# Two channels per kernel matmul in an S4 convolution kernel, with a new written order

## The chip, the cores and the metric

The kernel runs on one core of a Trainium2 chip. The metric is the device time of one execution in microseconds (us); the median of several runs is given with the lowest and the highest. One more execution was taken with the hardware profiler: its own time, its span (first to last instruction) and its trace are what is read here. The engines are called as the profile calls them: PE is TensorE (matmuls), PEld the weight loads of PE, DVE is VectorE, ACT is ScalarE, POOL is GpSimd, SP is SyncE, which issues most of the DMAs.

## The reference

The input `A_u` is 2048 rows of 512 channels. With `xn` the layer-normalised rows, the output is `x + s * g`:

```python
# _A_ref: long convolution, one kernel of 2048 taps per channel, 128 modes each
P = jnp.exp(logdA[:, :, None] * l[None, None, :])      # logdA = dt * (A_re + i A_im)
K = jnp.einsum("dn,dnl,dn->dl", Cc, P, dB).real
...                                                    # Kf, Uf: real FFTs of length 4096 of K and xn
Yf = Uf * Kf[None, :, :, :]
y = ...                                                # inverse FFT, first 2048 rows, + u * Dskip
# _B_ref: one row only goes through a gated layer
r = x @ w_r
idx = jnp.argsort(-r, axis=-1)[:, :C]                  # C = 1
y = (_silu(x_sel @ w_gate) * (x_sel @ w_up)) @ w_down  # times sigmoid of r at that row
return x + upd                                         # upd is y at that row, 0 elsewhere
...
x = A_u
xn = _layernorm(x, axis=-1)
s = _A_ref(xn, A_A_re, A_A_im, A_B_re, A_B_im, A_C_re, A_C_im, A_log_dt, A_Dskip)
g = _silu(_B_ref(xn, B_w_r, B_w_gate, B_w_up, B_w_down))
return x + s * g
```

## The kernel before

Everything is in SBUF, and the Fourier transforms are matmuls with constant tables.

*Front.* The rows arrive as X, are normalised (statistics on DVE, L791 and L794; XN on DVE, L815, or ACT, L814), and go out again and come back transposed as XZN by 16 DMAs on SP. XN is also written to a scratch tensor in DRAM, `scr_g`, from which the gate is read near the end. Beside it the parameters are loaded to STG and turned into weights: from sines and cosines SG, four products SL and two sums WC, 128x512 each, which PE turns over (PB<-DPF,WC) into MB. The forward transform of XN takes two steps, CB,XZN to AU and AU with F2A and F2B to BIG. A router picks one row; its gated layer streams weights through WRING, SMB and the small row GRW, which is added to `scr_g` at the chosen row by an indirect DMA on POOL.

*Kernel.* The 512 channels go in four quarters, called (h, s) in the code, 128 channels each. For a quarter, exponentials E and sines SN over 32 lags and powers GG over 20 base rows are made by ACT and DVE; `kgen_mm` multiplies them for each channel by itself: 32 columns of E (then of SN) as weights, 20 columns of GG moving, so 32 lags by 20 rows for one channel. Four channels sit side by side in the four column groups of the array, at (0, 32j). That is 256 matmuls a quarter and 1024 in all. KE takes them out of PSUM, and small matmuls (KE,CB) bring them to KX with the channels in order. `spec` multiplies KX by the table FD, 20 matmuls a group and 8 groups a quarter (KX,FD), KF takes a group out of PSUM (L624 on ACT, L625 on DVE), and DVE multiplies it into the spectrum of XN (BIG<-BIG,KF). FD is loaded in four parts of 8 of its 32 blocks, so each quarter uses the last part in its last two groups. `inv_a` is the first step back, with CB,BIG to CC.

*End.* `fin(h)` is the second step back, for half of the channels in five blocks: matmuls CC,FB, then DVE multiplies the block in PSUM with the gate, TB<-PB,G, adds the residual XR, and the block is stored. The gate G0 is read from `scr_g` after the chosen row is in it, and ACT makes it silu(gate) in four pieces (L591, G<-G).

*Order.* No engine picks its work at run time. `_Graph.op` records every operation with what it reads and writes; the table `ORDER` (L368) lists, for each engine, the numbers of its operations in the order in which they are issued; `schedule` puts them so and `emit` writes a semaphore wait where an operation needs another engine's or a DMA's. An evacuation of PSUM made by `evac` can stand on either ACT or DVE, whichever list has its number. Some helpers record many kinds of operation on one line: `mm` L642 all matmuls, `tt` L596 all two-input operations, `act` L591, `dma` L659, `memset` L628. A buffer's place in SBUF is fixed (RG, RM and so on are offsets), so two buffers at one place order each other.

Of the kernel before, what the change touches and what calls it, by code (L numbers as in the profile page):

```python
# [7 lines left out]
ACT = mybir.ActivationFunctionType  # L8
# [8 lines left out]
KB = 1024  # L17
# [310 lines left out]
def tables():  # L328
# [33 lines left out]
    for q in range(2):  # L362
# [11 lines left out]
        0-1 4 3 20 5 15 23-25 28 27 26 30-32 29 34 375 385 377 398-399 388 396 379 390-391 383 394 386 371 395 382 380 397 389 372 374 370 384 376
        393 378 392 387 400 373 381 49 48 50 47 175 36 44 51-52 403 58 133 131 134 412 53-54 57 55 76 56 75 46 416 405 81 79-80 82 425 433 427-428
        424 417 426 88 85 92 87 408 407 411 430 423 229 404 413 429 406 419 233 235 422 435 431 418 239 409 420 241 243 245 356 421 434 414 249 251
        253 255 257 259 432 410 415 263 265 267 269 271 584 583 273 275 277 279 615 601 605 281 283 491 285 287 593 494 289 291 661 293 591 611 613
        603 597 609 607 589 599 595 585 587 482 546 558 664 570 572 578 574-575 559-560 568 553 573 580 577 569 550 579 554 562 565 571 567 561 676
        566 555 557 556 552 563 576 564 551 608 755 752 594 616 590 598 586 588 610 758 596 612 604 592 606 602 600 614 764 685 767 549 770 332 689
        687 693 701-702 773 704 777 781 800 695 694 806 782-783 812 789-790 792 818 886 833 892 835 834 820 898 826 824 836 906 908 912 847 846 863  # L380
# [12 lines left out]
        889-890 895-896 822 901 893 902 838 842 839 841 899 840 844 904 851 910 858 845 865 859 866 873 852 874 921 914 922 915 928 935 929 936
        943-944""",
    gpsimd="""
        402 401 298 302 300 296 225 304 306 308 310 581-582 312 314 316 318 320 322 324 326 334 336 338 340 342 344 346 348 350 352 354 365""",
    tensor="""
        33 35 43 45 228 230 198-200 232 234 201 236 238 204 240 242 208 244 210 246 248 250 215 252 217 254 256 258 222 262 264 266 268 270 486 272
        274 487 276 278 490 488 280 282 489 284 286 226 493 288 290 660 292 537 297 299 538 541 301 303 539-540 663 666 544 672 669 678 305 675 307
        748 309 681 311 754 313 751 315 684 317 757 319 760 321 763 323 766 325 769 327 688 686 335 337 692 698 339 699 341 696 343 345 697 700 772  # L400
        347 703 349 776 351 793 353 780 355 799 360 690 796 774 805 778 784-785 788 811 802 786-787 808 791 814 879 882 817 885 888 891 894 821 900
        897 837 819 825 823 843 903 905 850 907 909 857 911 864 920 871-872 913 934 927 941-942""",
# [7 lines left out]
def build(nc, A_u, A_A_re, A_A_im, A_B_re, A_B_im, A_C_re, A_C_im, A_log_dt, A_Dskip,  # L410
# [51 lines left out]
    with g.ctx:  # L462
# [78 lines left out]
        E = g.buf("E", RE, [32, 256], BF16)  # L541
        SN = g.buf("SN", RS_, [32, 256], BF16)
# [12 lines left out]
        KE = [g.buf(f"KE{i}", RKE + 1280 * i, [20, 32], BF16) for i in range(2)]  # L555
# [351 lines left out]
        def exps(h):  # L907
            g.stage = f"exps{h}"
            hs = slice(256 * h, 256 * h + 256)
            for i in range(31):  # L910
                act(E(E.a[i]), AR(AR.a[hs]), ACT.Exp, scale=float(128 + LAGS[i]), table="exp")
            memset(PO, E(E.a[31]), 1.0)

        def sines(h):
            g.stage = f"sin{h}"
            hs = slice(256 * h, 256 * h + 256)
            th = TH(TH.a[hs])
            memset(PO, SN(SN.a[0]), 0.0)
# [322 lines left out]
```

## Time and profile before

| | |
|---|---|
| median of 3 runs, lowest, highest | 198.55 us, 197.79, 199.75 |
| the profiled execution's own time | 196.53 us |
| its span | 194.6 us |
| mean granted clock of PE | 0.891 |
| busy PE / PEld / DVE / ACT / POOL | 131.6 / 116.2 / 158.5 / 124.7 / 18.3 us |
| matmuls in the trace | 2960 |
| moved by DMA | 31.64 MB, mean 163 GB/s |
| bytes of instructions fetched (queue q8) | 23 packets, 0.38 MB |

Busy time is when at least one instruction of an engine was in work; register, branch and DMA-issuing instructions do not count. Matmuls overlap, so the mean of one (some 220 ns) is much longer than the distance between two, and busy time over count is the better measure. A granted clock of 0.50 means that PE was held to half speed in that stretch. The profile's groups read "line engine operation out<-in shapes xcount | busy, mean ns | idle before, releaser".

### The profile page before, as it was taken

Reading aid. Unit: us, or ns where it says so; the run is one execution under the profiler, and the core shown is the slowest. Engines: PE = TensorE matmul, PEld = TensorE weight load, DVE = VectorE, ACT = ScalarE, POOL = GpSimd, SP = SyncE. Lnnn points to the kernel's source line nnn. Section 1 sums busy time; section 2 is a strip of 40 time slices with the busy share of each in tenths; the row PEclk is TensorE's granted clock in tenths of the full one; section 3 lists DMA queues with packets and bytes.
Section 4 is the critical chain, followed back from the end, with each engine's and each line's share of the span. In section 5 each row is a group of like instructions: output and inputs, shape, how many; then the busy total and the mean of one; then the engine's idle time right before and its main releaser. Section 6 shows DMA issues by size and latency. Waiting matters only on the chain.

```text
span 194.6 us, 6818 instructions
## 1 busy us (share of the span) xinstructions
PE 131.6 (68%) x2960; PEld 116.2 (60%) x2960; DVE 158.5 (81%) x395; ACT 124.7 (64%) x246; POOL 18.3 (9%) x37
## 2 busy tenths in 40 slices
PE   0114040069786799935599997999999999958450
PEld 0003030069654567735589997989979899847330
DVE  0999998996799999991479999996947478949881
ACT  0699999994999969990099998243311339834000
POOL 6000000000002000022103433230010000000000
PEclk9999999999999979965599999856997999999755
DMA  5995069991000197999502444220296699980775
GB/s 162 383 384 236 2 132 149 159 389 38 0 0 2 19 308 177 331 365 301 121 0 76 129 132 126 84 88 20 59 229 153 205 421 316 201 158 20 158 150 121
DMA packets 24449, 31.64 MB, mean 163 GB/s; under 512 B 11012, under 2 KB 19332, under 8 KB 23652
## 3 DMA queue, kind: packets, MB, share of 16 engines
q1 hardware_dynamic: 16974, 22.79, 42.3%
q10 hardware_dynamic: 5958, 4.19, 9.5%
q0 software_dynamic: 1488, 4.23, 7.3%
q8 instruction: 23, 0.38, 0.8%
q14 instruction: 6, 0.05, 0.1%
HBM read 20.72 MB, written 4.20 MB: 128 GB/s over the span
## 4 chain that ended last, share of the span: by engine, by line
PE 40%; DVE 25%; ACT 15%; issue 8%; DMA 7%; SPq 2%; ACTq 0%
PE PB L642 40%; ACT E L591 5%; DVE TT L596 4%; DVE BIG L596 4%; DMA CF<-c_cf 4%; DVE GG L596 3%; DMA XZN<-XN 3%; DVE KF L625 3%; SPq L659 2%; DVE TB L596 2%; ACT BIG L624 2%; ACT XN L814 1%; ACT L591 1%; DVE E L596 1%; DVE AU L625 1%
## 5 line engine op out<-in xcount | busy, mean ns | idle before, releaser
L642 PE MATMUL PB<-KX,FD 128*128 128x128 bf16 x640 | 42.9, 229 | 0.7 <-DVE KF L625 0.5
L642 PEld LDWEIGHTS PB<-KX,FD 128*128 128x128 bf16 x640 | 39.7, 104 | 1.4 <-DVE KF L625 0.7
L596 DVE TENSOR_TENSOR TT<-GG,MB 128x512 bf16<-128x512 bf16 (+2 forms) x64 | 27.8, 462 | 0.1
L591 ACT ACTIVATE E<-AR 128x256 bf16<-128x256 f32 x62 | 19.4, 401 | 7.2 <-PE PB L642 7.2
L596 DVE TENSOR_TENSOR BIG<-BIG,KF 128x1024 bf16<-128x1024 bf16 x32 | 21.0, 685 | 2.7 <-issue 1.6
L642 PE MATMUL PB<-GG,SN 128*32 128x20 bf16 x512 | 19.7, 221 | 4.8 <-issue 4.8
L642 PE MATMUL PB<-CB,XZN 128*128 128x256 bf16 x64 | 11.7, 325 | 16.0 <-DMA XZN<-XN 13.4
L642 PE MATMUL PB<-GG,E 128*32 128x20 bf16 x512 | 19.7, 223 | 3.5 <-issue 3.2
L624 ACT ACTIVATE CC<-PB 128x1024 bf16<-128x1024 f32 (+1 forms) x14 | 12.4, 900 | 14.5 <-PE PB L642 14.5
L642 PEld LDWEIGHTS PB<-GG,E 128*32 128x32 bf16 x512 | 17.9, 167 | 5.7 <-issue 4.3
L642 PEld LDWEIGHTS PB<-GG,SN 128*32 128x32 bf16 x512 | 18.3, 169 | 4.5 <-issue 4.5
L642 PE MATMUL PB<-CB,BIG 128*128 128x128 bf16 x256 | 20.7, 240 | 0.5 <-ACT CC L624 0.3
L642 PEld LDWEIGHTS PB<-CB,BIG 128*128 128x128 bf16 x256 | 18.7, 153 | 1.4 <-issue 0.4
L642 PEld LDWEIGHTS PB<-CB,XZN 128*128 128x128 bf16 x64 | 8.5, 181 | 18.1 <-ACT MB L777 13.7
L596 DVE TENSOR_TENSOR GG<-TT 128x256 bf16<-128x256 bf16 (+2 forms) x66 | 18.1, 303 | 0.0
L625 DVE CAST KF<-PB 128x512 bf16<-128x512 f32 x17 | 11.6, 684 | 7.8 <-PE PB L642 7.8
L624 ACT ACTIVATE BIG<-PB 128x1024 bf16<-128x1024 f32 x16 | 15.7, 1059 | 1.8 <-PE PB L642 1.8
L624 ACT ACTIVATE KF<-PB 128x512 bf16<-128x512 f32 x15 | 8.9, 599 | 11.4 <-PE PB L642 11.3
L624 ACT ACTIVATE AU<-PB 128x1024 bf16<-128x1024 f32 x13 | 12.8, 1048 | 2.6 <-PE PB L642 2.6
L791 DVE BATCH_NORM_STATS2 ST<-X 128x6 f32<-128x512 bf16 x16 | 10.2, 673 | 4.3 <-DMA X<-in_A_u_dram 4.3
L596 DVE TENSOR_TENSOR TB<-PB,G 128x1024 bf16<-128x1024 f32 (+1 forms) x10 | 9.9, 1006 | 3.9 <-PE PB L642 3.9
L642 PE MATMUL PB<-DPF,WC 128*128 128x128 f32 x16 | 4.1, 441 | 11.2 <-DVE WC L596 11.2
(129 smaller groups left out, 240.2 us busy)
## 6 DMA issues: line engine op xcount, KB each, us to landing
FD<-c_fd SPq DMA_DIRECT2D x4, 1280.0 KB, 7.5
X<-in_A_u_dram SPq DMA_DIRECT2D x4, 512.0 KB, 5.5
XZN<-XN SPq DMA_DIRECT2D x16, 128.0 KB, 4.7
scr_g<-XN SPq DMA_DIRECT2D x4, 512.0 KB, 7.1
BIG<-BIG ACTq DMA_DIRECT2D x4, 512.0 KB, 6.7
G<-scr_g SPq DMA_DIRECT2D x1, 2048.0 KB
FB<-c_fb SPq DMA_DIRECT2D x1, 2048.0 KB, 15.7
XR<-in_A_u_dram SPq DMA_DIRECT2D x4, 512.0 KB, 13.4
```

Source lines behind the costliest of these rows:

```text
L591: g.op(AC, lambda e: e.activation(out=out.ap, in_=in_.ap, func=func, **kw), w=[out], r=r, cost=cost(AC, out, 0.834) - (20 if in_.buf.space ...
L596: g.op(eng, lambda e: e.tensor_tensor(out=out.ap, in0=a.ap, in1=b.ap, op=op), w=[out], r=[a, b], cost=cost(eng, out, rate))
L624: g.op(AC, lambda e: e.activation(out=out.ap, in_=in_.ap, func=ACT.Copy), w=[out], r=[in_], cost=cost(AC, out, 0.834) - 20, alt=(DV, lambd ...
L625: alt=(DV, lambda e: e.tensor_copy(out=out.ap, in_=in_.ap), cost(DV, out, 1.042)))
L642: ins = e.matmul(o_.ap, lhsT=l_.ap, rhs=r_.ap, start=st, stop=sp, **kw)
L659: fn = lambda e: e.dma_start(dst, src)
L791: g.op(DV, lambda e, b=b: e.bn_stats(ST6(ST6.a[b]).ap, X0(X0.a[b]).ap), w=[ST6(ST6.a[b])], r=[X0(X0.a[b])], cost=593)
L814: flex(ov, [iv, mv_, nv, rv], lambda e, ov=ov, iv=iv, nv=nv, rv=rv: e.activation(out=ov.ap, in_=iv.ap, func=ACT.Identity, bias=nv.ap, scal ...
```

## The change

The kernel's lines move by one or two: `mm` is L643, `tt` L597, `dma` L660, `evac` L625 and L626.

1. `kgen_mm` takes two channels in one matmul: 64 columns of E or SN (32 lags of two channels) as weights and 40 columns of GG (20 rows of the same two) moving. Half of each result is the product of unlike channels and is not used. There are 128 matmuls a quarter, 512 in all, at (0, 64jp). E and SN are laid out as [2, 32, 128], so that the columns are 64 elements apart (256 before). The results need twice the PSUM, so a quarter is made in two halves on the same two banks, each with its own KE evacuation; KE is one buffer for all quarters, and the matmuls KE,CB pick every second column of the identity to sort the channels.
2. The six products SL and WC are on POOL.
3. In `fin(1)` the blocks 0, 2 and 4 are copied by ACT from PSUM to YB in SBUF (bf16), and DVE multiplies from there.
4. XR lies where MB was (RM) and is recorded ahead of FB and G0; TB, V4, VM and YB lie where GG was. G0 comes in two loads, one for each half of the channels, and the silu pieces follow the halves.
5. All lists of `ORDER` are new. X comes first on SP. All 16 XN are on DVE (12 before, 4 were on ACT); all 16 AU evacuations are on ACT (13 before); of BIG's 16 evacuations one is on DVE; of KF's 32 casts 9 are on DVE (17 before).

PE first, where the first quarter's spectrum products meet the second quarter's kernel matmuls. Names: GG,E and GG,SN are the kernel matmuls, KX,FD the spectrum products, AU,F2B the second step of the forward transform. Before:

```order
L642 MATMUL PB<-AU,F2B 128x4x64 x16
L642 MATMUL PB<-KX_120,FD 128x2x64 x20
L642 MATMUL PB<-AU,F2B 128x4x64 x8
L642 MATMUL PB<-GG,E 32x20 x4
L642 MATMUL PB<-GG,SN 32x20 x4
```

and now, ahead of the first half of these kernel matmuls (the last two rows go on 16 times) the first fence, and at the end of the half, before the next, the second:

```order
L643 MATMUL PB<-KX_119,FD 128x2x64 x20
L643 MATMUL PB<-AU,F2B 128x4x64 x8
L643 MATMUL PB<-KX_119,FD 128x2x64 x20
L643 MATMUL PB<-AU,F2B 128x4x64 x16
L643 MATMUL PB<-GG,E 64x40 x2
L643 MATMUL PB<-GG,SN 64x40 x2
```

```order
L643 MATMUL PB<-GG,SN 64x40 x2
L643 MATMUL PB<-KX_119,FD 128x2x64 x20
L643 MATMUL PB<-AU,F2B 128x4x64 x8
L643 MATMUL PB<-KX_119,FD 128x2x64 x20
L643 MATMUL PB<-GG,E 64x40 x2
```

Before, one group of KX,FD stood ahead of the 256 kernel matmuls, which were broken only by the small matmuls of the router and the gated layer. Now two groups stand ahead of the first 64 and two between the halves; the other four follow the second half.

SP at the end of the program: the issue of the last loads. BIG is the exchange of spectrum halves, GRW the gated row, G the gate, FB the table of `fin`. Before:

```order
L659 DMA BIG<-BIG 64x2x1024
L659 DMA GRW<-UPD 8x1x64
L659 DMA G_132<-scr_g 128x8192
L659 DMA FB<-c_fb 128x8192
L659 DMA XR<-in_A_u_dram 32x32x256 x4
L659 DMA out_dram<-XR 32x8x128 x3
```

and now:

```order
L660 DMA BIG<-BIG 64x4096
L660 DMA XR<-in_A_u_dram 32x32x256 x4
L660 DMA BIG<-BIG 64x4096
L660 DMA GRW<-UPD 8x1x64
L660 DMA FB<-c_fb 128x8192
L660 DMA G_131<-scr_g 128x2x2048 x2
L660 DMA out_dram<-XR 32x8x128 x10
```

XR moved from the last of the loads to the first; FB stands between the gated row and the gate, which has two issues.

ACT near its end, where the gate's silu stands among the evacuations. CC and KF are evacuations of `inv_a` and `spec`. Before:

```order
L624 ACTIVATE CC<-PB 128x128x8
L624 ACTIVATE KF_123<-PB 128x512
L591 ACTIVATE G_132<-G_132 128x8x256
L624 ACTIVATE KF_125<-PB 128x512
L591 ACTIVATE G_132<-G_132 128x8x256 x2
L624 ACTIVATE CC<-PB 128x128x4
```

and now:

```order
L625 ACTIVATE KF_122<-PB 128x512
L592 ACTIVATE G_131<-G_131 128x2048 x2
L625 ACTIVATE CC<-PB 128x128x8
L592 ACTIVATE G_131<-G_131 128x2048
L625 ACTIVATE CC<-PB 128x128x4
```

Before, KF casts stood behind the first silu pieces; now all KF casts are ahead of them, and CC evacuations stand behind.

The diff, cut to its core (of the lists of `ORDER` the start of POOL's alone is shown; SN and the column helper `cols` follow E's layout in the same way):

```diff
 ORDER = dict(
...
     gpsimd="""
-        402 401 298 302 300 296 225 304 306 308 310 581-582 312 314 316 318 320 322 324 326 334 336 338 340 342 344 346 348 350 352 354 365""",
+        401-402 298 302 300 296 37-39 41 40 42 225 583-584 304 306 308 310 312 314 316 318 320 322 324 326 334 336 338 340 342 344 346 348 350 352
...
-        E = g.buf("E", RE, [32, 256], BF16)
-        SN = g.buf("SN", RS_, [32, 256], BF16)
+        E = g.buf("E", RE, [2, 32, 128], BF16)
+        SN = g.buf("SN", RS_, [2, 32, 128], BF16)
...
-        KE = [g.buf(f"KE{i}", RKE + 1280 * i, [20, 32], BF16) for i in range(2)]
+        KE = g.buf("KE", RKE, [2, 20, 32], BF16)
...
-        XR = g.buf("XR", RG, [32, 256], BF16)
-        V4 = g.buf("V4", RM, [512], BF16)
-        VM = g.buf("VM", RM + 1 * KB, [4, 512], BF16)
-        TB = [g.buf(f"TB{i}", RT + 2048 * i, [1024], BF16) for i in range(4)]
+        XR = g.buf("XR", RM, [32, 256], BF16)
+        V4 = g.buf("V4", RG + 8 * KB, [512], BF16)
+        VM = g.buf("VM", RG + 9 * KB, [4, 512], BF16)
+        TB = [g.buf(f"TB{i}", RG + 2048 * i, [1024], BF16) for i in range(4)]
+        YB = [g.buf(f"YB{i}", RG + 13 * KB + 2048 * i, [1024], BF16) for i in range(2)]
...
-        tt(DV, sl(0), sg(4), sg(2), ALU.mult)
-        tt(DV, sl(1), sg(5), sg(3), ALU.mult)
-        tt(DV, sl(2), sg(4), sg(3), ALU.mult)
-        tt(DV, sl(3), sg(5), sg(2), ALU.mult)
-        tt(DV, WC(WC.a[0].reshape(-1)), sl(0), sl(1), ALU.subtract)
-        tt(DV, WC(WC.a[1].reshape(-1)), sl(2), sl(3), ALU.add)
+        PP_ = PO
+        tt(PP_, sl(0), sg(4), sg(2), ALU.mult)
+        tt(PP_, sl(1), sg(5), sg(3), ALU.mult)
+        tt(PP_, sl(2), sg(4), sg(3), ALU.mult)
+        tt(PP_, sl(3), sg(5), sg(2), ALU.mult)
+        tt(PP_, WC(WC.a[0].reshape(-1)), sl(0), sl(1), ALU.subtract)
+        tt(PP_, WC(WC.a[1].reshape(-1)), sl(2), sl(3), ALU.add)
...
-                act(E(E.a[i]), AR(AR.a[hs]), ACT.Exp, scale=float(128 + LAGS[i]), table="exp")
-            memset(PO, E(E.a[31]), 1.0)
+                act(E(E.a[:, i]), AR(AR.a[hs].reshape(2, 128)), ACT.Exp, scale=float(128 + LAGS[i]), table="exp")
+            memset(PO, E(E.a[:, 31]), 1.0)
...
-            ke, kx = KE[qi % 2], KX[qi % 2]
-            lst = []
-            for c in range(32):
-                bank = PB[c // 16]
-                o_ = 20 * (c % 16)
-                for ri in range(2):
-                    for j in range(4):
-                        ch = 128 * s + 32 * j + c
-                        lst.append((bank(bank.a[o_:o_ + 20], 32 * j, 32), (E, SN)[ri]((E, SN)[ri].a[:, ch]), GG(GG.a[ri, :, ch]), ri == 0, ri == 1, (0, 32 * j)))
-                if c % 8 == 7:
-                    mm(lst, 18)
-                    lst = []
+            ke, kx = KE, KX[qi % 2]
             b0, b1 = PB[0], PB[1]
-            for ri in range(2):
-                a0 = cbo["PM"][0] + 4 * ri
-                lst.append((b0(b0.a[320:448], 0, 4), CB(CB.a[a0:a0 + 4]), PL(PL.a[ri, 128 * s:128 * s + 128]), ri == 0, ri == 1, None))
-            mm(lst, 60)
-            pv = PP[0].a.reshape(2, 512)[:, :320].reshape(2, 16, 20)
-            evac(ke(ke.a.reshape(20, 2, 16)), PP[0](pv.transpose(2, 0, 1)))
+            pv = PP[0].a.reshape(2, 512)[:, :320].reshape(2, 8, 40)
+            for ch_ in range(2):
+                lst = []
+                for cc in range(16):
+                    bank = PB[cc // 8]
+                    o_ = 40 * (cc % 8)
+                    for ri in range(2):
+                        for jp in range(2):
+                            ch = 32 * jp + 16 * ch_ + cc
+                            lst.append((bank(bank.a[o_:o_ + 40], 64 * jp, 64), (E, SN)[ri]((E, SN)[ri].a[s].reshape(64, 64)[:, ch]), GG(GG.a[ri, :, 128 * s + ch:128 * s + ch + 65:64].transpose(1, 0)), ri == 0, ri == 1, (0, 64 * jp)))
+                    if cc % 8 == 7:
+                        mm(lst, 28)
+                        lst = []
+                if ch_:
+                    for ri in range(2):
+                        a0 = cbo["PM"][0] + 4 * ri
+                        lst.append((b0(b0.a[320:448], 0, 4), CB(CB.a[a0:a0 + 4]), PL(PL.a[ri, 128 * s:128 * s + 128]), ri == 0, ri == 1, None))
+                    mm(lst, 60)
+                evac(ke(ke.a.reshape(40, 32)[:, 16 * ch_:16 * ch_ + 16].reshape(40, 2, 8)), PP[0](pv.transpose(2, 0, 1)))
...
-                    lst.append((bank(bank.a[o_:o_ + 160], 32 * a, 32), CB(cb("IDB")[32 * j:32 * j + 32]), ke(ke.a[5 * a:5 * a + 5].reshape(160)), True, True if a else None, (0, 32 * a)))
+                    lst.append((bank(bank.a[o_:o_ + 160], 32 * a, 32), CB(cb("IDB")[64 * (j % 2) + j // 2:64 * (j % 2) + 64:2]), ke(ke.a[j // 2, 5 * a:5 * a + 5].reshape(160)), True, True if a else None, (0, 32 * a)))
...
+        YV = (0, 2, 4)
...
-                tt(DV, tv, pr(pv[:, :w_].reshape(2, nr, 64).transpose(1, 0, 2)), G0(G0.a[a2, 2 * h:2 * h + 2, b0:b0 + nr].transpose(1, 0, 2)), ALU.mult)
+                src = pr(pv[:, :w_].reshape(2, nr, 64).transpose(1, 0, 2))
+                if h and kb in YV:
+                    y_ = YB[kb % 2]
+                    yv = y_(y_.a[0:2 * w_].reshape(nr, 2, 64))
+                    act(yv, src, ACT.Copy)
+                    src = yv
+                tt(DV, tv, src, G0(G0.a[a2, 2 * h:2 * h + 2, b0:b0 + nr].transpose(1, 0, 2)), ALU.mult)
...
+        g.stage = "ldr"
+        for p_ in range(4):
+            load(XR(XR.a.reshape(-1), 32 * p_, 32), _dma_rows(A_u, 16384 * (p_ // 2) + 256 * (p_ % 2), [[32768, 32], [512, 32], [1, 256]]), 32 * 16384)
         g.stage = "ldz"
         load(FB(FB.a.reshape(-1)), t_fb.ap(), 128 * 16384)
         g.stage = "ldg"
-        load(G0(G0.a.reshape(-1)), dram(SCRG, 0, [[8192, 128], [1, 8192]]), 128 * 16384, tokr=[f"scrg{a}" for a in range(4)] + ["row"])
-        g.stage = "ldr"
-        for p_ in range(4):
-            load(XR(XR.a.reshape(-1), 32 * p_, 32), _dma_rows(A_u, 16384 * (p_ // 2) + 256 * (p_ % 2), [[32768, 32], [512, 32], [1, 256]]), 32 * 16384)
+        for h in range(2):
+            load(G0(G0.a[:, 2 * h:2 * h + 2].reshape(2, 2048)), dram(SCRG, 2048 * h, [[8192, 128], [4096, 2], [1, 2048]]), 128 * 8192, tokr=[f"scrg{a}" for a in range(4)] + ["row"])
         g.stage = "fpre"
         for bb in range(4):
-            gv = G0(G0.a[:, :, 4 * bb:4 * bb + 4].reshape(8, 256))
+            gv = G0(G0.a[bb % 2, 2 * (bb // 2):2 * (bb // 2) + 2].reshape(2048))
...
```

More of the change, by code (lines that the diff above doesn't have):

```diff
@@ L373 @@
+        875 874 883 882 881 873 929 923 931 924 947 945-946 938 940 956 955""",
     scalar="""
[L374 to L376 removed]
@@ L377 @@
[L377 to L380, printed above, removed]
@@ new lines @@
+        0 2 4 13 19-20 16 23-26 28 27 32 30-31 29 34 399 393 400 398 397 395 394 383 396 384 391 380 377 386 374 390 385 373 388-389 379 375 370 392
+        376 382 372 378 381 371 387 36 47 50 48-49 51 403 52 44 424 57 56 422 427 423 412 405 53 429 54 407 413 420 411 409 431 75-76 404 410 425 58
+        415 82 81 434 55 419 85 88 87 421 433 417 430 426 428 229 231 418 233 432 435 416 235 237 239 241 243 245 247 249 251 253 255 257 259 414
+        406 408 263 265 267 269 586 585 271 356 589 597 601 599 488 275 277 587 595 492 279 281 609 495 283 607 605 285 287 663 289 291 613 666 540
@@ new lines @@
+        615 603 669 482 611 617 672 293 591 593 592 612 596 594 544 598 678 545 610 608 602 675 604 547 606 616 588 614 590 600 618 575 554 581-582
+        557 568 571 559-560 563 558 566 755 580 573 555 553 687 761 565 564 569 764 574 567 570 556 572 562 577 767 579 578 689 561 576 691 552 773
+        770 693 695 697 700 332 776 704 778 705 780 784 801 798 807 813 786 782 816 824 794 826 796 885 894 897 900 903 906 838-839 909 840 915 841
+        917 865 868 872 880 919 932 930 925 922 934 944 950 939 937 954 953""",
@@ new lines @@
+        272 486 274 276 490 489 491 278 280 226 494 282 284 662 286 665 288 290 538-539 668 292 671 541 543 542 297 299 301 303 677 674 546 683 680
+        754 751 305 307 688 686 309 757 760 311 763 313 315 766 317 690 769 319 772 692 321 323 694 325 698-699 327 775 701-703 777 335 337 779 339
+        706 783 341 800 797 343 345 806 803 347 812 809 781 818 815 788 349 351 353 355 823 360 787 821 790 792 791 827 825 795 829 884 887 890 893
+        896 899 842 902 905 848 910 908 855 914 912 862 916 869 876-877 926 918 941 933 948-949""",
@@ L917, in sines @@
             th = TH(TH.a[hs])
-            memset(PO, SN(SN.a[0]), 0.0)
+            memset(PO, SN(SN.a[:, 0]), 0.0)
             act(THA(), th, ACT.Abs)
@@ L923, in sines @@
                 act(CO(CO.a[j - 1]), THA(), ACT.Sin, scale=-8.0 * j, bias=pi2, table="silu", tokr=["set"])
-                act(SN(SN.a[15 + j]), th, ACT.Sin, scale=8.0 * j, table="silu", tokr=["set"])
+                act(SN(SN.a[:, 15 + j]), TH(TH.a[hs].reshape(2, 128)), ACT.Sin, scale=8.0 * j, table="silu", tokr=["set"])
         def cols(h, s):
@@ L930, in cols @@
             cs = slice(128 * s, 128 * s + 128)
-            sn, ee, co = SN.a[:, cs], E.a[:, cs], CO.a[:, cs]
+            sn, ee, co = SN.a[s], E.a[s], CO.a[:, cs]
             pair = lambda x: x[1:31].reshape(2, 15, 128)[:, 0:8]
```

36 lines of the change are left out of this document (15 added, 21 removed).

## The prediction

> **What bounds the kernel now.** I began with the page: busy times, the 40 slices (one slice is 4.87 us) and the chain's shares.
>
> ```profile
> span 194.6 us, 6818 instructions
> PE 131.6 (68%) x2960; PEld 116.2 (60%) x2960; DVE 158.5 (81%) x395; ACT 124.7 (64%) x246; POOL 18.3 (9%) x37
> PE   0114040069786799935599997999999999958450
> DVE  0999998996799999991479999996947478949881
> ACT  0699999994999969990099998243311339834000
> PEclk9999999999999979965599999856997999999755
> DMA  5995069991000197999502444220296699980775
> PE 40%; DVE 25%; ACT 15%; issue 8%; DMA 7%; SPq 2%; ACTq 0%
> ```
>
> DVE is the busiest by the total, but the stages differ: up to slice 8 DVE and ACT are full and PE waits; from slice 20 to 34 PE is full. In slices 16 to 19 PE, DVE and ACT all fall while DMA stays at 9. The chain of waits shows what that hole is:
>
> ```profile
> 84.53 3.23 issue
> 87.75 2.88 PE PB L642 x128
> 90.63 3.87 issue
> 94.50 4.10 PE PB L642 x56
> ...
> 171.78 2.43 issue
> ```
>
> "issue" is time in which PE waited for nothing that the profile shows. The times by stretch, cut at those holes (PE, PEld, DVE, ACT, POOL busy with counts, clock, DMA share, GB/s), and the queue that carries instructions, tell what it is:
>
> ```profile
> 70.33:84.54 14.21, 13.70 (x382) 10.59 (x382) 13.76 (x41) 12.95 (x22) 0.97 (x2) 0.86 0.89 276
> 87.74:90.64 2.90, 2.88 (x128) 2.58 (x128) 0.48 (x1) 0.16 (x1) 1.07 (x2) 0.50 1.03 325
> 94.49:171.79 77.30, 75.18 (x1659) 70.89 (x1659) 64.80 (x136) 45.33 (x86) 11.69 (x22) 0.89 0.55 147
> 90.64:94.49 3.85, 0.00 (x0) 0.00 (x0) 0.00 (x0) 0.00 (x0) 0.00 (x0) 0.50 1.05 237
> q8 instruction: 23, 0.38, 0.8%
> ```
>
> Between two holes PE ran exactly 128 matmuls, before that 382 (3 x 128, two records missing), after it 1659 (13 x 128, five missing). A matmul is two instructions, so holes come only every 256; an instruction packet is 0.38 MB / 23 = 16.5 KB, 64 bytes for each of 256. So PE waits there for its own program: after the resume at 87.75 the next block came only at 94.50, 6.75 us later, while the DMA engines were full (share 1.03 and 1.05) and the 128 small matmuls lasted 2.9 us. Where the DMA share is 0.55, thirteen borders passed unseen. From 94.49 to 171.79 PE is busy 75.2 of 77.3 us: PE-bound. The end is a ping-pong of PE and DVE (waits from 163 on):
>
> ```profile
> PE PB L642 <- DVE TB L596: 4.1, 5, 1.3
> DVE TB L596 <- PE PB L642: 3.9, 4, 2.6
> ```
>
> The profiled execution took 196.53 us (span 194.6); the median of the runs is 198.55, 1.0% above. I sum against 196.53 and scale at the end.
>
> **The change, part by part.**
>
> *Kernel matmuls (kgen_mm).* 1024 matmuls of 32 columns by 20 become 512 of 64 by 40.
>
> ```profile
> L642 PE MATMUL PB<-GG,E 128*32 128x20 bf16 x512 | 19.7, 223 | 3.5 <-issue 3.2
> L642 PE MATMUL PB<-GG,SN 128*32 128x20 bf16 x512 | 19.7, 221 | 4.8 <-issue 4.8
> L642 PEld LDWEIGHTS PB<-GG,E 128*32 128x32 bf16 x512 | 17.9, 167 | 5.7 <-issue 4.3 <-DVE E L596 0.4 <-DVE GG L596 0.4
> L642 PE MATMUL PB<-KX,FD 128*128 128x128 bf16 x640 | 42.9, 229 | 0.7 <-DVE KF L625 0.5 <-ACT KX L624 0.2
> L642 PE MATMUL PB<-CB,BIG 128*128 128x128 bf16 x256 | 20.7, 240 | 0.5 <-ACT CC L624 0.3
> 88.60:90.40 1.80, 1.80 (x109) 1.80 (x110) 0.00 (x0) 0.00 (x0) 1.07 (x2) 0.50 1.01 338
> 125.75:126.30 0.55, 0.55 (x33) 0.55 (x32) 0.55 (x2) 0.00 (x0) 0.10 (x1) 0.50 0.01 0
> ```
>
> Two stretches of nothing but these matmuls give 1.80/109 = 16.5 ns and 0.55/33 = 16.7 ns each: 1024 x 16.7 = 17.1 us. No 64x40 row exists here. If the pitch is per instruction it stays 16.7 (8.5 us in all); if it goes with the columns, 33.3 (17.1, nothing gained); the far end is the 128-column strided load, 20.7/256 = 81 ns in busy time. I take 25, midway between the two near ends: 512 x 25 = 12.8, 4.3 less PE. Half of it counts, -2.1 (bounds: -8.6 with 16.7 and all on the path, +17.0 in rival B), since the evacuations that follow keep their lengths and still set when a bank comes free.
>
> *Instruction blocks.* 512 matmuls fewer are 1024 instructions, four blocks of 23. The order also puts FD products among the kernel matmuls. KX,FD costs 42.9/640 = 67 ns each in its row, so a block of 64 kernel matmuls (1.6 us), 40 KX,FD (2.7) and 24 of the narrower AU,F2B at half that (0.8) lasts about 5 us, against 6.75 between requests: about 1.8 per border at most in full DMA. The holes cost 3.23 + 3.87 = 7.1 on the chain; I leave 1.0: -6.1 (-7.1 to -3.5, two borders at 1.8). The hole at 171.78 came from 128 borders lining up with the short matmuls of fin; with other counts the border moves into longer work: -2.4, and 0 if it falls on fin again. The Trainium skill, "Runtime: NRT & Kernel Launch", section "Instruction fetch mechanics", agrees on 256 instructions a block but calls the cost of a border mostly hidden. This trace disagrees under a full DMA (3.23 and 3.87 us); by the page the holes would have another cause, the term would be 0 and the sum that of rival A.
>
> *Casts and copies between engines.*
>
> ```profile
> L625 DVE CAST KF<-PB 128x512 bf16<-128x512 f32 x17 | 11.6, 684 | 7.8 <-PE PB L642 7.8
> L624 ACT ACTIVATE KF<-PB 128x512 bf16<-128x512 f32 x15 | 8.9, 599 | 11.4 <-PE PB L642 11.3
> L625 DVE CAST AU<-PB 128x1024 bf16<-128x1024 f32 x3 | 3.6, 1214 | 0.0
> L815 DVE TENSOR_SCALAR XN<-X,LST 128x512 bf16<-128x512 bf16 x12 | 4.1, 408 | 0.0
> L814 ACT ACTIVATE XN<-X,LST 128x512 bf16<-128x512 bf16 x4 | 3.0, 798 | 0.0
> L596 DVE TENSOR_TENSOR SL<-STG 128x512 f32<-128x512 bf16 x4 | 2.7, 684 | 0.0
> L596 DVE TENSOR_TENSOR BIG<-BIG,KF 128x1024 bf16<-128x1024 bf16 x32 | 21.0, 685 | 2.7 <-issue 1.6 <-ACT KF L624 0.9
> L596 DVE TENSOR_TENSOR TB<-PB,G 128x1024 bf16<-128x1024 f32 x6 | 7.2, 1218 | 3.2 <-PE PB L642 3.2
> L591 ACT ACTIVATE G<-G 128x2048 bf16<-128x2048 bf16 x4 | 7.5, 1908 | 0.2 <-DMA G<-scr_g 0.2
> 34.06 6.26 DMA XZN<-XN
> ...
> L642 PE MATMUL PB<-CB,XZN 128*128 128x256 bf16 x64 | 11.7, 325 | 16.0 <-DMA XZN<-XN 13.4 <-ACT AU L624 1.3 <-DVE AU L625 0.7
> ```
>
> Eight KF casts go from DVE to ACT: DVE loses 8 x 0.684 = 5.5 us, ACT gains 8 x 0.599 = 4.8, in a stretch of 77.3 us where ACT is busy 45.3 and DVE 64.8. With shorter PE work DVE would be next to bound this stretch; the chain has DVE 25%, ACT 15%, so I let half of ACT's 4.8 count: -2.4 (0 to -5.5). KE is evacuated in two halves and the second half's matmuls wait in PE's queue for the first: four more evacuations of about a KF cast's 0.6 us, 2.4, with other products put between the blocks: +0.5 (0 to +2.4). Three AU evacuations (1.214 each on DVE) come to ACT and four XN at 0.798 leave it: I let these cancel.
>
> *The front.* X is loaded first, all normalisations go on DVE (four more at 0.408, +1.6), six products leave it (6 x 0.684 = -4.1): DVE -2.5 ahead of XZN's loads, which the chain has at 34.06. How long the products take on GpSimd no row shows. If nobody waits for them, -2.5. If each blocks DVE for its own time, bounded by 0.684 (DVE's row) and 1.908 (the longest elementwise row, ACT's), six cost 4.1 to 11.4: +1.6 to +8.9. I take -1.0, nearer the good end: what they feed is weights for PE, and PE waits 13.4 us for XZN there, which covers them. The Trainium skill, "SBUF — State Buffer", section "Who interferes with whom", speaks against the move: a DVE instruction with two SBUF inputs and a GpSimd one that reads SBUF exclude each other for the whole instruction. No GpSimd tensor row is in this trace; it is rival C.
>
> *The end.* In fin(1) ACT copies three blocks to SBUF, so DVE's product need not read PSUM: two of 1.218 fall to 0.685 (BIG's row, the same width from SBUF) and one of half width saves less: -1.3 of DVE, and PE's bank is free after ACT's copy instead of DVE's product. PE waited 4.1 us for TB: -1.5 (0 to -4.1).
>
> XR is loaded ahead of FB and G now; G comes in two halves, behind the gated branch's row (GRW) and FB on SP. The four gate activations are 4 x 1.908 = 7.6 on ACT. The first two stand in its queue ahead of CC evacuations that fin's matmuls need, so a late row blocks ACT, then PE. G's load was waited for only 0.2 us: I take 0, and up to +3 if the shorter PE work ahead leaves the branch last.
>
> Sum: -1.0 - 2.1 - 6.1 - 2.4 - 2.4 + 0.5 - 1.5 = -15.0. 196.53 - 15.0 = 181.5; times 198.55/196.53 = 183.4, so 183.
>
> **The rivals.**
>
> *A, the data binds where the program did.* In the holes the DMA engines were full with loads that the spectrum products need, too:
>
> ```profile
> L659 SPq DMA_DIRECT2D FD<-c_fd x4: 365/376/606, 66.3 to 81.6; - x4
> DMA to landing us min/median/max: 7.2/7.5/13.2
> ```
>
> The last FD load was issued at 81.6 and may land up to 13.2 later, 94.8: when PE resumed. If PE waits for FD instead of instructions, the 6.1 is lost: 187.6, scaled 189.5. For it: a DMA share of 1.05 in the hole, and the same bytes to move. Against it: this part serves only the last two of the first quarter's eight spectrum groups, and in the new order all of that quarter's kernel matmuls and the next one's stand ahead of these two.
>
> *B, slower: the wide weight load takes longer.* Load rows show 167 ns for a 32-column strided load and the pitch is the same at clock 0.50 in both stretches, so something other than the array sets it, perhaps four column groups loading side by side: 4 x 16.7 = 67 ns for four. Were only two 64-column loads to fit where four fit now, with each twice as long, a matmul takes 67 ns: 512 x 67 = 34.1, 17.0 more than now, all of it on a PE that is 97% busy in its long stretch. The other terms make -12.9: 196.53 + 17.0 - 12.9 = 200.6, scaled 202.7. It decides from 17.1/512 + 12.9/512 = 59 ns a matmul upward. Against it: nothing of that kind is needed if the pitch is per instruction, and the four times wider load of CB,BIG, 20.7/256 = 81 ns a matmul with 128 moving columns, sets a ceiling near 40 for half its columns.
>
> *C, GpSimd blocks DVE.* At 1.3 us, the middle of 0.684 and 1.908, six are 7.8: 7.8 - 2.5 = +5.3 in place of -1.0, so 187.8, scaled 190; at the far end, +8.9, 193.5.
>
> **How the numbers follow.** The forecast has 0.62, at 183, with its own range 177 to 189: below, kernel matmuls at 16.7 ns and no wait for TB at the end, -4.8; above, two borders at 1.8 (+2.6), the late gate (+3), no gain of KF (+2.4), not all at once. A has 0.18 (189.5), C 0.08 (190), B 0.09 (203), and 0.03 is for what I don't see. The range for 8 in 10 runs from 175 to 196: B lies outside, with a few cases of the forecast below. About 1% is what a measurement of this kernel can tell from no change. Faster by more, under 196.6: forecast, A and C, less the cases in which A or C meets the late gate and lost terms, 0.83; within 1%: 0.07; slower: B and a little more, 0.10.
>
> **What would show it.** The kernel matmuls' 64x40 rows: a pure stretch at 25 ns right, 60 or more is B. The chain should have no "issue" over 2 us; 128 matmuls between any that are left would keep the mechanism. Under A, PE waits for "DMA FD". Under C the DVE rows between 10 and 25 us grow beyond 0.69 and GpSimd's products stand beside them. KF casts 9 on DVE, and DVE busy near 150. At the end PE's wait for TB should be under 3 us; a wait of ACT for G's load of over 2 us would be the late gate. Wrong altogether if the hole of slices 16 to 19 stays with no PE name on it.

## The result: slower, 1.062 of the time before

The changed kernel takes 212.34 us (median of 4 runs, 209.30 to 213.82), the kernel before 198.17 (197.27 to 199.75). The ratio is 1.062, 95% interval 1.045 to 1.078. The prediction said 183 and faster. The profiled execution took 209.30 us, its span is 207.5. Runs in a slower state of the machine are left out of every ratio: here two of the four (the others took 209.30 and 211.83), and in one group of experiments (marked below) most runs of the kernel before and two of one kernel, so that the four kernels of that group are set beside 188.03 us, the time of the version that they start from.

The page of the changed kernel, its totals, slices and chain shares:

```profile
span 207.5 us, 5797 instructions
PE 153.2 (74%) x2448; PEld 135.1 (65%) x2448; DVE 154.2 (74%) x386; ACT 130.4 (63%) x255; POOL 33.5 (16%) x43
PE   0114300099866999999999998999999999977641
PEclk9999999999999655797979999555799559999965
q8 instruction: 19, 0.31, 0.7%
PE 50%; DVE 17%; ACT 15%; DMA 11%; SPq 2%; issue 2%; POOL 0%; DVEq 0%; ACTq 0%
```

PE lost 512 matmuls and gained 21.6 us of busy time. The hole of slices 16 to 19 is gone, the instruction packets fell from 23 to 19 as forecast, and the chain's "issue" fell from 8% to 2%. In exchange PE is full from slice 14 on, and the granted clock has more and longer half-speed stretches.

Where the 12.9 us between the two spans lie is read from the times by stretch, cut at the first kernel matmul and at the first matmul of `fin` (PE, PEld, DVE, ACT, POOL, clock, DMA share, GB/s). Before, then changed:

```profile
66.45:168.66 102.21, 92.18 (x2172) 84.36 (x2173) 83.00 (x193) 61.86 (x118) 13.89 (x26) 0.85 0.63 180
168.66:194.60 25.94, 13.20 (x586) 10.90 (x584) 17.61 (x25) 5.45 (x6) 0.00 (x0) 0.77 0.65 128
```

```profile
67.05:183.20 116.15, 114.61 (x1664) 104.17 (x1664) 78.79 (x188) 62.24 (x127) 16.62 (x27) 0.78 0.60 168
183.18:207.50 24.32, 12.69 (x586) 10.45 (x584) 17.30 (x25) 12.87 (x11) 0.00 (x0) 0.82 0.43 90
```

The front is 0.6 us longer (67.05 against 66.45), the end 1.6 shorter, the middle 13.9 longer. In the middle PE's idle time fell from 10.0 to 1.5 us (7.1 of it the removed holes), while its busy time rose by 22.4. That rise has two parts. Two stretches of nothing but kernel matmuls in the changed kernel, one at half and one at full clock, and the groups:

```profile
74.40:78.40 4.00, 4.00 (x64) 4.00 (x64) 0.91 (x2) 1.67 (x4) 0.00 (x0) 0.50 0.40 87
97.70:99.70 2.00, 2.00 (x32) 2.00 (x32) 1.33 (x3) 1.98 (x4) 0.00 (x0) 1.00 0.95 286
...
L643 PE MATMUL PB<-KX,FD 128*128 128x128 bf16 x640 | 43.9, 233 | 0.6 <-ACT KF L625 0.5
L643 PE MATMUL PB<-CB,BIG 128*128 128x128 bf16 x256 | 23.8, 261 | 2.2 <-DVE CC L626 0.9 <-DVE BIG L597 0.8 <-ACT CC L625 0.5
L643 PE MATMUL PB<-AU,F2A 64*128 64x256 bf16 x84 | 8.3, 345 | 2.6 <-ACT BIG L625 1.4 <-ACT AU L625 1.2
```

A wide kernel matmul takes 4.00/64 = 62.5 ns at either clock, and 65 between the starts of neighbours in a run; 512 x 65 = 33.3 us against 17.1: 16.2 more. And the other matmuls beside them are slower: KX,FD, CB,BIG and AU,F2A together 76.0 us, where they were 70.2 before (42.9, 20.7 and, in the row below, 6.6), with the clock of the middle at 0.78 instead of 0.85.

```profile
L642 PE MATMUL PB<-AU,F2A 64*128 64x256 bf16 x84 | 6.6, 298 | 2.5 <-ACT BIG L624 1.4 <-ACT AU L624 1.1
```

So 16 us of dear matmuls and 6 of slowed neighbours, less 8.5 of holes and waits, make the 13.9 to within half a microsecond.

### The profile page after: what moved, and what is told of

Same layout as the page of the kernel before. It is cut to its first block, busy times and chain, and to the rows that moved or that the text cites. A ratio compares the mean times of both kernels' runs of the same rounds, so it can differ in the third digit from the quotient of the medians.

```text
span 207.5 us, 5797 instructions
## 1 busy us (share of the span) xinstructions
PE 153.2 (74%) x2448; PEld 135.1 (65%) x2448; DVE 154.2 (74%) x386; ACT 130.4 (63%) x255; POOL 33.5 (16%) x43
## 4 chain that ended last, share of the span: by engine, by line
PE 50%; DVE 17%; ACT 15%; DMA 11%; SPq 2%; issue 2%; POOL 0%; DVEq 0%; ACTq 0%
PE PB L643 50%; ACT E L592 4%; DMA WRING<-in_B_w_down_dram 4%; ACT AU L625 4%; DVE ST L793 3%; DMA X<-in_A_u_dram 3%; DVE TB L597 3%; DMA XZN<-XN 3%; DVE XN L817 3%; SPq L660 2%; ACT BIG L625 1%; ACT KF L625 1%; ACT CC L625 1%; DVE XR L597 1%; DVE MR L597 1%
## 5 line engine op out<-in xcount | busy, mean ns | idle before, releaser
L643 PE MATMUL PB<-KX,FD 128*128 128x128 bf16 x640 | 43.9, 233 | 0.6 <-ACT KF L625 0.5
L643 PEld LDWEIGHTS PB<-KX,FD 128*128 128x128 bf16 x640 | 40.7, 105 | 2.5 <-ACT KF L625 1.0
L643 PE MATMUL PB<-GG,E 128*64 128x40 bf16 x256 | 34.2, 320 | 0.0
L643 PE MATMUL PB<-GG,SN 128*64 128x40 bf16 x256 | 33.9, 319 | 0.0
L643 PEld LDWEIGHTS PB<-GG,E 128*64 128x64 bf16 x256 | 29.3, 225 | 2.4 <-issue 1.6
L643 PEld LDWEIGHTS PB<-GG,SN 128*64 128x64 bf16 x256 | 29.7, 228 | 0.0
L597 DVE TENSOR_TENSOR BIG<-BIG,KF 128x1024 bf16<-128x1024 bf16 x32 | 21.7, 687 | 9.3 <-ACT KF L625 9.1
L597 DVE TENSOR_TENSOR TT<-GG,MB 128x512 bf16<-128x512 bf16 (+2 forms) x64 | 27.7, 463 | 0.0
L643 PE MATMUL PB<-CB,BIG 128*128 128x128 bf16 x256 | 23.8, 261 | 2.2 <-DVE CC L626 0.9
L625 ACT ACTIVATE KF<-PB 128x512 bf16<-128x512 f32 x23 | 13.5, 594 | 15.3 <-PE PB L643 15.3
L643 PEld LDWEIGHTS PB<-CB,BIG 128*128 128x128 bf16 x256 | 21.1, 156 | 3.0 <-DVE CC L626 1.0
L643 PE MATMUL PB<-MR,XZN 128*128 128x64 bf16 x64 | 6.1, 259 | 19.1 <-DMA XZN<-XN 19.1
L625 ACT ACTIVATE CC<-PB 128x1024 bf16<-128x1024 f32 (+1 forms) x15 | 12.6, 851 | 9.9 <-PE PB L643 9.9
L643 PEld LDWEIGHTS PB<-MR,XZN 128*128 128x128 bf16 x64 | 6.1, 214 | 19.5 <-DMA XZN<-XN 19.4
L597 DVE TENSOR_TENSOR GG<-TT 128x256 bf16<-128x256 bf16 (+2 forms) x66 | 18.1, 304 | 0.0
L625 ACT ACTIVATE AU<-PB 128x1024 bf16<-128x1024 f32 x16 | 15.4, 1049 | 3.1 <-PE PB L643 3.0
L884 POOL DMA_INDIRECT GX<-scr_g,SMI x1 | 9.5, 9494 | 39.9 <-DVE SMI L607 39.9
L625 ACT ACTIVATE BIG<-PB 128x1024 bf16<-128x1024 f32 x15 | 14.7, 1027 | 2.0 <-PE PB L643 2.0
L625 ACT ACTIVATE KE<-PB 128x640 bf16<-128x640 f32 x6 | 4.2, 699 | 13.9 <-PE PB L643 13.9
L592 ACT ACTIVATE SN<-TH 128x256 bf16<-128x256 f32 x32 | 11.3, 402 | 2.5 <-PE PB L643 2.5
```

The source lines that it names most:

```text
L592: g.op(AC, lambda e: e.activation(out=out.ap, in_=in_.ap, func=func, **kw), w=[out], r=r, cost=cost(AC, out, 0.834) - (20 if in_.buf.space ...
L597: g.op(eng, lambda e: e.tensor_tensor(out=out.ap, in0=a.ap, in1=b.ap, op=op), w=[out], r=[a, b], cost=cost(eng, out, rate))
L625: g.op(AC, lambda e: e.activation(out=out.ap, in_=in_.ap, func=ACT.Copy), w=[out], r=[in_], cost=cost(AC, out, 0.834) - 20, alt=(DV, lambd ...
L643: ins = e.matmul(o_.ap, lhsT=l_.ap, rhs=r_.ap, start=st, stop=sp, **kw)
L884: g.op(PO, lambda e: e.indirect_dma_start(out=GX(None, 0, 8).ap, out_offset=None, in_=rows, in_offset=bass.IndirectOffsetOnAxis(ap=SMI(Non ...
```

## The experiments

The theory after the result: what a kernel matmul costs is set by loading its weight columns, which lie 64 elements apart (W). Rivals: the 40 moving columns, 512 bytes apart, set it (M); a 64-column tile is slow in itself (T); or the new order and the moved loads are slow, whatever the matmul.

### The matmul alone

A kernel of blocks of 64 matmuls of one form on idle engines, with wide matmuls between the blocks; it holds nothing of the reference's work.

```diff
+config("WB", 64, 64, 2, "G2")    # 64 columns, 64 elements apart, two tiles, 40 moving (as changed)
+config("WP", 32, 256, 1, "G20")  # 32 columns, 256 apart, one tile only, 20 moving
+config("WQ", 64, 64, 1, "G2")    # 64 columns, 64 apart, one tile only
+config("WN", 128, 64, 0, "G2")   # 128 columns, 64 apart, the whole array
```

> A kernel that holds none of the reference's work: blocks of 64 matmuls of one form each, with 12 wide matmuls (128x512) ahead of each block, on otherwise idle engines. The blocks differ in the number of weight columns, the distance between them, the column tiles in use and the moving columns. Theory W (weight columns): a strided column costs a fixed time in its own column group, some 2.1 ns, and groups load side by side; so 32 columns at distance 256 on four tiles take 16.7 ns a matmul, 64 at distance 64 on two tiles 65 ns, with 20 moving columns as with 40; on one tile 67 and 130 ns; contiguous columns take well under 20 ns in all forms. Theory M (moving columns): the 64-column form takes 65 ns with 40 moving columns and about 33 with 20, whatever the distance of the weight columns. Theory T (tile form): 64-column tiles take 65 ns with contiguous columns too.

The groups of four of its 18 blocks, in the order WP, WQ, WN, WB (busy us, mean ns of one):

```profile
L418 PE MATMUL PB<-M,W 128*32 128x20 bf16 x64 | 4.4, 220 | 0.0
L418 PEld LDWEIGHTS PB<-M,W 128*32 128x32 bf16 x64 | 4.3, 169 | 0.7 <-issue 0.7
...
L418 PE MATMUL PB<-M,W 128*64 128x40 bf16 x64 | 8.5, 319 | 0.0
L418 PEld LDWEIGHTS PB<-M,W 128*64 128x64 bf16 x64 | 8.4, 228 | 0.8 <-issue 0.8
...
L418 PE MATMUL PB<-M,W 128*128 128x40 bf16 x64 | 7.2, 304 | 0.0
...
L418 PE MATMUL PB<-M,W 128*64 128x40 bf16 x64 | 4.8, 328 | 0.0
```

The distance between two is (busy - mean)/63. On one tile 32 columns take 66 ns and 64 columns 130, some 2.05 ns a column at distance 256 and at 64 alike; so four tiles side by side gave 16.7 in the kernel before, and two give 65. In the two-tile block it is 71. With 20 moving columns it was 64, so theory M falls for the wide form; with neighbouring columns 43, so T falls, though W had said under 20. With the columns 8, 32 and 128 elements apart the wide form took 60, 63 and 65 ns. The blocks WN and WQ hold a surprise: 128 columns at distance 64 on the whole array take 109 ns, less than 64 columns on one tile. That is 0.86 ns a column against 2.05, so a tile's load can't be scaled down from that of the full array. The narrow form did not reach 16.7 here on its four tiles: it took 27 ns, 19 with neighbouring weight columns, and 14 with the weights 256 apart as before but neighbouring moving columns. So for the narrow form the place of the moving columns counts too, which none of the three theories had; for the wide form it was not tried. Only the one-tile blocks agree with theory W to a few per cent.

The Trainium skill, "TensorE: Matmul & The Clock Gate", section "LDWEIGHTS (loading the stationary operand)", gives a load as columns/1.2 in ns. By estimate that is 27 and 53 ns for 32 and 64 columns; the one-tile blocks show 66 and 130, so for columns that are apart on a column tile the measurement says 2.4 to 2.5 times as much.

### Changed kernel, narrow matmuls

```diff
-for jp in range(2):   # 64 columns, 40 moving, at (0, 64 * jp)
+for j in range(4):    # 32 columns, 20 moving, at (0, 32 * j)
```

> The changed kernel with the kernel matmuls back at one channel each (1024 of 32 columns by 20), everything else as changed, the KE evacuation in two halves included. Under the theory that the wide matmul alone made the loss: 16.7 ns a matmul, so 33.3 - 17.1 = 16.2 us less than the 209.3 of the profiled execution, about 193, and down to 188 where the half-clock stretches around the kernel matmuls shrink with them. Rival, the fetch holes come back with the 1024 instructions: up to 7 more, 195 to 200. Rival, the order or the moved loads are slow in themselves: above 200.

204.21 us, 1.035 of before (1.025 to 1.046). Its profiled execution took 204.35 us, so only 5 of the 16 us came back. That is above the 195 to 200 of the rival with the holes, and in the range of the rival that blamed the order. The chain decides for the holes:

```profile
120.39 4.18 PE PB L643 x171
124.57 4.66 issue
129.23 3.90 PE PB L643 x119
133.13 3.30 issue
136.43 18.81 PE PB L643 x377
...
155.24 2.87 issue
```

Holes of 4.66, 3.30 and 2.87 us, where the changed kernel has none in the middle; between the first two the times by stretch count 128 matmuls. They stand at other places than before and add up to 10.8 us, where the three before made 9.5. The sum closes with them: 209.3 - 16.2 + 10.8 = 203.9. That the order is not slow in itself the next run shows, which has the same order.

### Changed kernel, neighbouring weight columns

```diff
-(E, SN)[ri].a[s].reshape(64, 64)[:, ch]   # 64 apart
+(E, SN)[ri].a[s].reshape(64, 64)[ch]      # next to each other, values of other lags
```

> The changed kernel, but each kernel matmul reads its 64 weight columns from 64 neighbouring elements (the values are those of other lags and channels; counts, sizes and everything else stay). Theory W: under 25 ns a matmul, 512 x 40 = 20 us less PE work, so about 188. Theories M and T: 65 ns and 209 as before.

184.85 us, 0.938 of before (0.930 to 0.946). Nothing but the place of the weights (and so their values) differs from the changed kernel, so the loss of the change is the place of the weights. A stretch of kernel matmuls, the groups, and the clock in 40 slices:

```profile
71.00:73.00 2.00, 2.00 (x64) 2.00 (x58) 2.00 (x8) 2.00 (x4) 0.00 (x0) 1.00 0.99 319
...
L643 PE MATMUL PB<-KX,FD 128*128 128x128 bf16 x640 | 39.5, 221 | 1.6 <-DVE KF L626 1.4 <-ACT KX L625 0.2
L643 PE MATMUL PB<-CB,BIG 128*128 128x128 bf16 x256 | 20.9, 238 | 3.8 <-issue 1.8 <-DVE CC L626 0.9 <-DVE BIG L597 0.8
L643 PE MATMUL PB<-AU,F2A 64*128 64x256 bf16 x84 | 6.0, 271 | 2.6 <-ACT BIG L625 1.4 <-ACT AU L625 1.2
...
PEclk9999999999999999999999999975999999999555
```

The distance between two is not under 25 ns, as I expected, but 35 between the starts of neighbours (31 by the stretch): 17.9 us in all, no less than the 17.1 of the narrow form; what sets the 35 is open. The half-clock stretches beside the kernel matmuls are gone, and the three neighbours fell to 66.4 us, 9.6 less than in the changed kernel. The slow weight loads cost twice here: 33.3 - 17.9 = 15.4 us themselves, and 9.6 in the neighbours, with the clock; together 25.0, where the profiled executions (209.30 and 185.14 us) differ by 24.2. One half-clock stretch is left in the middle, behind a hole that has come back:

```profile
120.25 1.84 issue
```

### Changed kernel, 20 moving columns

```diff
-GG(GG.a[ri, :, 128 * s + ch:128 * s + ch + 65:64].transpose(1, 0))
+GG(GG.a[ri, :, 128 * s + ch])   # the products of the second channel are left out
```

> The changed kernel, but each kernel matmul moves 20 columns (one channel) instead of 40; the products for the second channel are left out. Theory W: still 65 ns a matmul, 209 us. Theory M: 33 ns, 16 us less, about 193.

208.40 us in a single execution, beside the 209.30 of the changed kernel's profiled one; the starts are 61 ns apart. Theory M falls in the kernel too.

### A layout that has the columns together and right

```diff
-E = g.buf("E", RE, [2, 32, 128], BF16)      # lag, channel
+E = g.buf("E", RE, [2, 64, 32, 2], BF16)    # channel, lag, half of the quarter
-act(E(E.a[:, i]), AR(AR.a[hs].reshape(2, 128)), ACT.Exp, ...)
+act(E(E.a[:, :, i]), AR(AR.a[hs].reshape(2, 2, 64).transpose(0, 2, 1)), ACT.Exp, ...)
...                                          # SN, CO and the column helper in the same way
```

> The changed kernel with E, SN and CO laid out channel by channel, so that the 64 weight columns of a kernel matmul lie next to each other and hold the right values; ACT writes them in pieces of two elements, DVE works in runs of 14 to 32. The weight-column theory gives 35 ns a kernel matmul, as in the run with wrong values, and 184 to 186 us if the ACT and DVE operations on the new layout keep their times (408 and 402 ns, 678 ns for 128x1024). If DVE loses its double rate on short runs, its 20 us on E and SN become up to 36 and half of that shows: 192. If ACT pays for pieces of two elements, 94 operations grow from 0.4 to up to 0.8 us: up to 200.

188.03 us, 0.950 of before (0.944 to 0.957). This one computes all that the reference asks for, and beats both kernels. DVE kept its times; ACT pays for the scattered pieces, as the rows of E in the changed kernel and in this one show:

```profile
L592 ACT ACTIVATE E<-AR 128x256 bf16<-128x256 f32 x62 | 19.9, 405 | 0.0
```

```profile
L592 ACT ACTIVATE E<-AR 128x256 bf16<-128x256 f32 x62 | 23.6, 470 | 0.0
```

0.065 us on each of 126 operations (E, SN and CO; I had left CO out of the 94) is 8 us of ACT. The time is 3 us above the 184.85 of the run with wrong values. That these 3 come from ACT is not shown: the three neighbours took 68.8 us in this profiled execution and 66.4 in that one.

### One thing at a time on that layout

The other runs start from this version. The products back on DVE (`PP_ = DV`, their numbers moved to DVE's list):

> The same, and the six products back on DVE, spread among the statistics of the normalisation. If GpSimd kept DVE waiting as much as it freed it, or more (rival C of the prediction): 0 to 6 us faster than with the products on GpSimd. If nothing waited for them: DVE has 6 x 0.68 = 4.1 us more ahead of the transposing loads, 2 to 4 us slower.

189.50 us, 0.961 (0.954 to 0.969) beside 0.950 (0.944 to 0.957): 1.5 us slower, and the intervals overlap a little. Rival C has no support; the move to GpSimd gains 1.5 us by the medians, 0 to 3 with their spread, and less than the 2 to 4 expected. The row of the changed kernel's GpSimd shows what a product takes, inside rival C's bounds:

```profile
L597 POOL TENSOR_TENSOR SL<-STG 128x512 f32<-128x512 bf16 x4 | 4.5, 1149 | 9.6 <-DMA STG<-in_A_C_re_dram 9.6
```

The narrow matmuls on the new layout, weight columns 2 elements apart:

```diff
+(E, SN)[ri].a[s][ch % 64, :, ch // 64]   # 32 columns, 1024 matmuls
```

> The channel-by-channel layout of E, SN and CO with the kernel matmuls of one channel (1024 of 32 columns at distance 2, 20 moving): the same PE time for the kernel matmuls as the wide ones on this layout (17 to 19 us against 17.9), but 1024 instructions more. If the number of instructions makes the holes: 'issue' gaps of 1 to 5 us between groups of 128 matmuls come back, and 10 to 15 us on the 188 of the wide form, 198 to 203. If the distance of the weight columns made the slow clock and with it most of the loss: 188 to 192.

196.60 and 199.04 us (this and the three kernels after it are the marked group), 8.6 to 11 more than the wide form. Its profiled execution, at 203.13 us longer than these two, has holes of 5.97, 4.24, 3.33 and 3.24 us, with 128 matmuls counted between the first two. Half of the kernel matmuls in that trace:

```profile
L643 PE MATMUL PB<-GG,E 128*32 128x20 bf16 x512 | 12.7, 206 | 10.9 <-issue 10.9
```

The same row of the kernel before has 19.7 busy. 123 of them in a stretch of 1.10 us (86.30 to 87.40) are 9 ns each, where 256 apart they took 16.7; all 1024 come to some 10 us, and I had expected 17 to 19. So with the weight columns 2 elements apart the narrow ones cost PE less than the wide ones' 17.9, and lose it to the holes. The number of instructions is what the wide form saves, not PE's time.

THA in the order in which CO is written:

```diff
-act(THA(), th, ACT.Abs)
+act(THA(THA.a.reshape(2, 64, 2)), TH(TH.a[hs].reshape(2, 2, 64).transpose(0, 2, 1)), ACT.Abs)
```

> The wide form on the channel-by-channel layout, with THA kept in the order in which CO is written, so that the 32 operations of CO read neighbouring elements and still write pieces of two. If the scattered read is what made ACT's operations 0.07 us longer, CO falls from 478 to about 414 ns a piece, 2 us less of ACT and 0 to 2 us of the total; if it is the write, nothing changes.

CO's operations fell from 478 to 422 ns, so it is the scattered read that made them longer; the time is 189.13 us (188.40 to 190.81), no gain on 188.03.

SP's tail as before, XR last:

```diff
-696 834 832 831 833 785 363 835-837   # BIG, XR x4, BIG, GRW, FB, G x2
+696 785 363 836-837 835 834 832 831 833
```

> The wide form on the channel-by-channel layout with the tail of SP's queue as it was before: both BIG, the gated row, the gate, FB, and XR last. If the place of XR, FB and the gate bears on the end: 1 to 4 us slower, and DVE or PE wait for XR or FB. If it bears on nothing: the same within 1%.

201.02 us (199.34 to 201.80), 13 slower, where I had expected 1 to 4. The waits from 155 us on:

```profile
PE PB L643 <- DMA FB<-c_fb: 7.3, 1, 7.3
...
DVE XR L597 <- DMA XR<-in_A_u_dram: 4.3, 1, 4.3
```

7.3 + 4.3 = 11.6 of the 13 us are waits for loads that the moved lines had taken out of the end. The chain runs through the loads of XR: two of their four issues held SP for 10.24 and 5.70 us. In the kernel before no wait for FB or XR is on record: FB landed at 152.1 + 15.7 = 167.8 us, just ahead of the first matmul that reads it at 168.7.

Without ACT's copies to YB (`YV = ()`):

> The wide form on the channel-by-channel layout without ACT's copies to YB: DVE multiplies all blocks of fin(1) from PSUM. By the prediction's term the copies are worth 1.5 us (0 to 4): so 1.5 slower; if ACT's copy only takes the place of DVE's longer product in the chain of PE and DVE: the same within 1%.

189.05 us (187.81 to 190.21) beside 188.03 (187.08 to 189.51): 1.0 slower, which lies between the two expectations, and the ranges overlap. So this run can't tell 1.5 us from nothing. The end, from the first matmul of `fin`, takes 24.7 us in this profiled execution and 24.2 in that of the version with the copies.

## Why the prediction was wrong, point by point

- **The step that failed** is the price of a wide kernel matmul: "I take 25, midway between the two near ends". It is 65: the kernel matmuls, forecast to take 4.3 us less of PE, took 16.2 more. Both near ends (16.7 per instruction, 33.3 per column) came from the pitch of the narrow form, which is one quarter of a load (66 ns on one tile), since four tiles load side by side. The LDWEIGHTS rows of the kernel before had hinted at it: 167 ns for 32 strided columns, and for 128 columns

```profile
L642 PEld LDWEIGHTS PB<-CB,BIG 128*128 128x128 bf16 x256 | 18.7, 153 | 1.4 <-issue 0.4 <-ACT CC L624 0.4 <-DVE BIG L596 0.2
```

With two tiles in place of four and each load twice as long (130 ns on one tile), the pitch is four times as long, not twice.
- **Rival B** had this mechanism and its number (67 ns). I gave it 0.09, by the argument that CB,BIG's 81 ns for 128 columns "sets a ceiling near 40 for half its columns". That argument is wrong: a full-array load is not a sum of column tiles (109 ns for 128 columns, 130 for 64 on one tile, at the same distance).
- B's sum, 200.6 for the profiled execution, was still 8.7 short of 209.30. Some 6 of it goes with the clock: I had read that the pitch of the kernel matmuls does not depend on it, but not that the half-clock stretches stand where the kernel matmuls are, and that longer ones would slow the work beside them. The rest is the front and the end, below.
- **The holes.** Right in the mechanism, and more than forecast: -7.1 of the middle against -6.1. Part of that is the slow matmuls themselves, which leave more time for the fetch: with the columns together and the same order, a hole of 1.84 us is back. Blocks of 128 matmuls are shown from the other side by both runs with narrow matmuls. The holes begin after 727, 855 and 2514 recorded matmuls before, 2386 in the changed kernel, 1236 with neighbouring columns, and 1492, 1620 and 2003 in the changed kernel with narrow matmuls; all are 82 to 87 past a multiple of 128. That speaks against rival A. The hole of the end stayed, 1.70 us at 198.02 (2.43 before), where I had -2.4.
- **The front.** -1.0 forecast, +0.6 measured. X comes first, but the four loads take 9.0 us to land where they took 5.5; the transposing loads are issued from 25.4 to 35.1 (24.3 to 34.1 before).
- **The end.** -1.5 and -2.4 forecast; the end is 1.6 shorter, 0.7 of it the hole, and the share of the copies to YB could not be told from nothing.
- **XR and the gate**, put at 0: right for the kernel before, but in the kernel with cheap weights this move, FB's place included, is worth 12 us. I priced it against today's PE, not against the shorter one that the other terms made.
- **KF casts, KE halves**: no run tells them apart from the rest.
- The sum without the kernel matmul's term was -12.9: 183.6 for the profiled execution. With the columns together, whose kernel matmuls cost 0.8 more than before, it took 185.14, where 183.6 + 0.8 is 184.4. About 4 of the us gained, the neighbours' 70.2 less 66.4, go with the clock, which was in no term; so the agreement is in part luck.

## What to carry to other kernels

Before matmuls are made wider, take one tile's load by itself from the trace (columns, distance, how many tiles share the array), for the pitch of a tiled stream hides the overlap, and here a full-array load said nothing of a tile's. Where weights are small, try their columns next to each other, even if the engine that writes them pays for it. Count the instructions too: with the columns together, the narrow matmuls cost PE the least and lost it again to holes. And price a moved load against the kernel that the other changes will make: what hides it now may be what they remove.

## What the runs showed of the hardware

- A weight column that is 64 or 256 elements from the next takes about 2 ns on a single column tile (130 ns for 64 columns, 66 for 32), and the pitch of the wide matmul in the kernel is the same at full and at half clock (62.5 ns). Tiles of different columns load side by side: four tiles of 32 columns (4 x 16.7 ns) take as long as one (66).
- 64 columns on two tiles: 65 ns a matmul when 64 elements apart, 35 when together. 32 columns on four tiles: 16.7 ns when 256 apart, 9 when 2 apart. 128 columns on the whole array, 64 apart: 109.
- In the changed kernel the clock was halved during and behind long stretches of slow strided matmuls, two to four us after their start, and not beside the same number of matmuls with their columns together. What in them halves it is open: in the kernel of the matmul alone the clock fell to 0.50 right behind some blocks of such matmuls (71, 65 and 63 ns) and not behind others (64 and 60 ns).
- 1024 instructions more on PE cost 8.6 to 11 us in the same order and layout, and 19 (204.2 against 184.9) where the columns are apart as well. They go with holes at borders of 128 matmuls. The DMA engines were full or nearly so in some of these holes (shares of 1.02, 1.05 and 0.91 before, 1.21 with narrow matmuls) and not in others (0.61 and 0.03), so a full DMA alone does not explain them.
